# Turning queries and keys with the DMA crossbar in a fused attention and long-convolution kernel

## The chip, the core and the metric

The kernel runs on one core of a Trainium2 chip. The core has five engines with an instruction queue each: TensorE (PE in the profile; PEld is its weight load), VectorE (DVE), ScalarE (ACT), GpSimd (POOL) and SyncE (SP). Each executes its queue in order and waits on semaphores. POOL and SP also issue DMAs: POOL through a software queue, which may convert types on the way, and SP through a hardware queue. Both run on the same 16 DMA engines. The metric is device time in microseconds (us). The time before is 175.86 us, the median of three runs (175.34 to 179.3).

## What is computed

Batch 4, 8 heads, 768 positions, head size 64. The attention sees 8 global keys and a window of 96 keys back, with a bias by distance for each head. Its output, as 512 columns, passes through a gated convolution of the whole length (a Fourier transform in the reference):

```python
scores = scale * (q @ k.T) + bias          # bias = -slope[h] * distance
scores = where(keep, scores, -1e9)         # first 8 keys, or 0 <= row - col < 96
x = softmax(scores) @ v                    # (B, S, 512)
x1, x2, x3 = split(x @ w_proj)             # 512 columns each
conv = irfft(rfft(x2, axis=1) * rfft(filter_fft, axis=0))
out = ((x1 * conv * x3) @ w_out)
```

## The kernel before, in words

**Stages.** For each batch there are two parts. `attention(b)` turns queries and keys, computes scores, exponentials, masks and products with the values, normalises and turns the result into `xT`, and computes the gates (L1098) from it. `conv(b)` projects (L1159), transforms forward (L924), multiplies by the filter's spectrum, transforms back (L1181, L1184), joins with the gates and projects to the output (L1215). The work of `conv(b)` is interleaved with that of `attention(b + 1)`.

**Who sets the order.** The kernel does not leave its order to a compiler. `Plan` collects operations with their engines, estimated costs and the keys that they read and write. `lay` places them one after the other by rank, `NUDGES` shifts each operation's rank and its leaning between ACT and DVE by a stored number, and `FAVOUR` is a leaning of all. `fill` puts idle matmuls (L563, on a tile of zeros) into gaps that PE is planned to have. `program` merges the five planned lines into one program order, and `emit` writes it out. The plan knows only dependencies named by keys. When the program is written, the layer below adds the semaphore waits that it finds necessary from the memory that the instructions touch, in program order.

**Loading.** Queries, keys and values are loaded by POOL (L583), converted from 32 to 16 bits, one tile at a time: a query tile is 128 positions in `qn`, a key tile 120 positions in partitions 8 to 127 of `kn`, and a value tile likewise in `vn`. There is one `qn` and one `kn`, so the next batch's tile is loaded when the last one has been used. Of the order of a batch: query tiles 0 to 2, key tiles 0 and 1, value tiles 0 and 1; query tiles 3 and 4, key tiles 2 and 3, value tiles 2 and 3; then query tile 5, key tiles 4 to 6 and value tiles 4 to 6. Batch 0 is loaded in another way (`load_pair`) and turned by `transpose_pair`; the change does not touch its turning.

**Turning.** For batches 1 to 3, `transposes` (L931) turns a tile: four 128x128 PE transposes (L938) into one PSUM bank, then a copy by ACT or DVE (L567) into 128 columns of `QT`, or into 120 columns of the 128 that a key tile has in `KT`. The first eight columns of each of the seven key tiles hold the eight global keys. They are written by a DVE copy of their own (L949 to L951), once for each batch, which spreads the eight first keys of tile 0 over all seven tiles:

```python
g.op("V", dve(224), lambda _: self.copy(
    "V", kv[:, :, :, 0:NG], kv[:, :, 0:1, NG:2 * NG].to_broadcast([P, 4, 7, NG])),
    r=[("KT", 0)], w=["KTg"])
```

**Scores.** `scores` (L953) of a group of key tiles (0 and 1; 2 and 3; 4 to 6) for two heads reads the key tiles of its group, the query tiles they meet, and `KTg` (matmuls L975). ACT takes the exponential (L990), DVE multiplies by the mask (L997), and `values` (L1015, L1020) follows. `load_global` (L662) copies the eight global rows of the value tile for the other tiles, by SP.

**SP's queue** holds two loads of batch 0, those small value copies and the 25 output stores (L1221).

Of the kernel before, what the change touches and what calls it, by code (L numbers as in the profile page):

```python
# [17 lines left out]
NG = 8  # L18
# [46 lines left out]
class Plan:  # L65
# [90 lines left out]
    def lay(self):  # L156
# [84 lines left out]
        830, 19469, 28342, 22698, -36791, 44557, 0, 38863, 17326, 50370, 0, 17086, -14969, 46246, -10719,  # L241
        3803, 22479, 12714, -995, -27474, -4380, 3973, 17122, 3529, 7380, -663, -24781, -3497, 45666, -4551,
        -35801, 10005, 0, 12791, 0, -10379, 0, 45454, 0, -5437, 0, -14061, -19757, -14504, -37905, -18946,
        0, -32477, 0, -19819, 0, 19446, -1510, 8329, 0, 27319, 11852, 7297, -33522, -3329, -24534, -36612,
        -27852, 3113, -7029, -29691, -14381, -3884, 31147, 32034, 41013, 3882, -7384, -6372, -2549, 6629,
        68912, 8963, -61766, 5547, -44599, 12091, 18399, 14042, 6929, -4982, -7955, 13539, -24252, 20179,
        -37287, 999, -15997, -18090, 9312, 22827, 23386, 28496, -25966, 23940, -7783, 39729, 0, 1069, 0,
        12644, 0, -10150, 0, 23681, 0, -18062, 0, -19460, 0, 7837, 0, 430, 0, -3637, 0, 8913, 0, -4969, 0,
        4698, 0, 6387, -28901, -14115, 14320, -44762, 8724, -14864, 46735, -14488, 23611, -14772, -11847,
        6451, -3306, -18377, -60, 4689, 27298, 24083, -497, -18877, 16900, 19934, 37256, 19651, -14734,  # L250
        -9560, 12718, -42257, 27146, 1115, -39200, -14114, 6946, -5667, 16361, -49626, -3804, -7768, -67026,
        -18259, 60927, 21512, -46061, 5299, 29871, 21514, -44548, 5866, -12730, -23878, -15725, 33821,
        20215, -25471, 41707, 6771, 23796, 39844, 27531, -14231, -2302, -5026, 6456, 8053, 1663, -7662,
        -1658, -22536, 10581, -5577, -28542, -40863, -38468, -5794, -5468, 40622, -19008, 14370, 67736,
        -58861, 42786, 25155, -29878, -3418, 3618, 4708, -22659, -28259, -20518, 8701, 6031, -6892, -10351,
        -20996, 26804, 20150, 54288, -13311, 5794, 6136, 52867, -15428, -29665, 25192, 30956, 45334, 21269,
        43306, 2557, -24451, 6157, -1880, -4325, -2390, 7965, -31500, -28218, 18854, 4142, 15094, -27249,
        27912, 43510, -17851, -24582, -28451, 3289, -4573, 52435, 13404, 20792, -24567, 15357, -28602,
        -63577, -4124, -16002, 20822, -14047, -23587, 29959, -35143, 9243, -7310, -76644, -8134, 42347,
        15822, -12242, -3646, -30686, 275, 21750, -36005, 1469, 29713, -50088, -42560, -19350, 23864, 5050,  # L260
        -35144, 35778, -23119, -25177, 16491, -2020, 4380, -36451, -22654, -22150, -20473, 13426, -26733,
        26609, 6268, -22149, 3957, -50217, -3909, -19153, 2810, -3292, 7853, -21492, 32509, 30392, 1058,
        -3422, 15580, -35441, -9203, -35466, 64502, 42951, -19116, -24283, 2677, -62640, -12510, -59703,
        11602, 21513, 35378, 20196, 11922, -1695, 2261, 5554, -11981, 15156, 12890, -23779, -19040, -49831,
        -15466, -43761, 7442, 2473, -11475, -562, -20186, 44257, -33302, -12882, -28759, 38437, 11482, 1330,
        11240, -38355, 17055, 27903, 51476, 19276, 41100, -22953, 19243, -49765, 30962, -35331, 10963,
        42827, 51939, -23434, -11212, 50785, -4094, -27838, -30215, -24532, -12422, 67855, 13805, 3349,
        -31574, -50206, -1578, -23241, 3462, -29661, 8300, 12759, 26155, 16907, 2610, 5092, 33120, -6934,
        14181, -6832, 37905, -14123, 4017, -27020, -20812, 1598, 3482, -15360, 14795, 14629, 485, 23373,
        31416, -26303, 985, -32770, -12960, -31274, -27569, 14995, 28878, -62352, -24591, -25434, -13467,  # L270
        -1753, 33337, -31036, -11856, -18317, -11803, -33535, -27683, -51311, -11621, 1840, -23345, -13880,
        -10610, -21888, -29421, -35794, 9291, 16111, -10016, -61858, 13788, 28430, 11863, 10235, 26016,
        -11573, 27177, -20634, 32822, -31295, 24126, 16224, 34719, 32835, 36139, 40036, 830, 39163, 18794,
        23592, 7759, 51877, 15207, 11097, 5209, -31196, 47785, 18050, 12543, -18408, 3112, 9419, 28821,
        33481, 24315, -4637, -2954, 58662, 10982, 44569, -17852, -13026, 18502, 18480, 661, 39608, 43043,
        5607, -6149, 51251, -23733, 21791, 22094, 13091, 28673, -13130, 38566, 29894, 58869, 14114, 22687,
        13217, 23944, 14851, 18542, 32490, 39556, 0, 2287, 0, 19051, 0, -4358, 0, -11746, 0, 19030, -37967,
        1328, 0, -1449, 14563, -17652, -982, -19950, 0, -1349, 0, -11190, 0, 2329, 0, 1474, 0, 9498, 0,
        18549, 0, 6688, 0, 22215, 0, 20539, 0, 3845, 0, 18493, 0, -9540, 0, 5625, 0, -4323, 0, -8046, -3533,
        -19460, 16225, 5133, -15664, 1868, -10430, 13679, -822, -6032, 46722, 17, -12126, -14344, -697,  # L280
        -13742, -12505, 35119, 19976, 12563, -17553, -4315, -16313, -8060, -26919, -13513, 5645, -9234,
        -8261, 33619, 1834, -2859, -2550, 21273, 8957, -13081, -9314, 20868, 8922, -5132, 5559, 6221,
        -35799, 24500, 3519, -6685, 3949, -816, -6213, 9623, -62952, -17310, 10679, 22559, -35498, 10601,
        -12029, 6157, 5514, 7375, -48803, 10526, -28598, 4222, -27669, -30984, 26626, 10987, -54583, -53116,
        -15825, 15071, -78852, -9661, 6714, 2840, -38629, -19587, -4267, 24678, -95876, 18875, -65326,
        37035, -57223, 2718, -80355, 8544, -25562, 24290, -40863, 2118, -56826, 1618, -8022, -31710, 24818,
        3620, -25827, 27844, -44889, 2870, 4692, 1799, -40217, -9884, -31044, -26859, 10139, -30260, 15490,
        -10550, -33083, -6484, -3536, 42406, -39070, 25617, -4598, 29316, -41708, 15965, 36737, 22936,
        -38817, 8527, -48993, 22443, 17760, 28836, -35248, -5369, -32024, 12970, -29506, 46391, 21693,
        -7287, -24248, -581, -2018, 24139, -49992, 23604, -37246, -19201, -50818, 32705, -650, -7523, -9491,  # L290
        -6925, -30680, 1857, -10661, 4404, 11499, 32387, -17435, -48594, -14949, -4657, -84287, -8566,
        14498, -17867, 2527, 39846, -8706, -27278, 52664, 6571, -35366, -320, -10331, -13919, -41255,
        -14510, -27402, 30994, -7841, -31169, -15489, 10258, -20175, 13543, 2857, 2578, 131, -1314, -20053,
        -3100, 4481, -24160, -39099, 11687, -27948, -9199, -2494, 30419, -9029, -805, -6822, -33325, 13405,
        -16820, -66296, -481, -11964, 10636, -6248, -15247, -30087, 9838, -10144, -26515, -24439, -29855,
        -22320, -23621, -44190, -16823, -1332, 20402, -52166, -32146, 29136, -8657, -32420, -27767, 19595,
        4945, -41783, -6152, 22710, -839, 24762, 12982, -46639, 45086, -32249, -27885, 26993, 32349, -1139,
        -27028, 5428, -35713, -11537, -21816, 4520, 11355, -11306, -17012, 4480, -2042, -15007, 18089,
        16310, 5551, -12842, -12327, -74283, -24015, -51377, 27730, -6713, 30891, -54126, 34332, -19745,
        -18476, -68884, 4160, 17961, -25458, -47047, -23408, -74718, -25716, -25378, 10363, -21807, -25577,  # L300
        -30760, -512, -35125, -15528, 5905, 11983, -39028, 8438, -56403, -744, -68035, -9455, -28679, 15786,
        -55653, 8176, -11569, -5453, 4461, 21051, 30451, 38894, -23961, -22340, -37283, -19384, -14914, 91,
        -24447, -19426, -32077, 21216, 6861, -6808, -6892, 5217, 10775, -14628, 70698, 20491, 17063, -9496,
        43779, -27379, 19441, -35221, 40472, -6558, 6850, 27498, 19585, 24533, 14892, -3738, -53050, 27975,
        -49714, -29727, 2330, -4593, -32440, 10709, 5615, -11179, -8091, 16512, -42979, 22940, -7459,
        -19376, -58359, -5155, 3527, 14869, 75937, 14885, 50802, -44287, 9855, -3550, 31325, 23170, 11445,
# [1108 lines left out]
```

## Time and profile before

| | |
|---|---|
| median of three runs | 175.86 us (175.34 to 179.3) |
| the profiled execution | 177.28 us |
| its span in the profile | 175.5 us |
| PE busy | 166.9 us, 95% |
| DVE busy | 157.0 us, 89% |
| ACT busy | 152.6 us, 87% |
| POOL busy | 75.3 us, 43% |
| four-matmul transposes of `qn` and `kn` (L938) | 156 matmuls between 38 and 112 us |
| idle matmuls (L563) | 16, all before 12 us |
| first and last score matmuls of batch 1 | 41.7 and 60.7 us |

Times inside the profile are counted from the start of the span. The busy time of PE includes the drain of pipelined matmuls, so a PE that is shown busy may still have room. "Idle before, releaser" in a line of a group is the time that its engine stood idle before these instructions, and what ended it. DMA share above 1 means that packets of several transfers were under way on an engine at once. "To landing" is the time from the start of the instruction that issues a DMA to its completion.

### The profile page before, as it was taken

To read this page: it belongs to the slowest core of one execution; us is meant where nothing else is said; L and a number is where in the kernel's file an instruction comes from. 1 tells how busy PE (TensorE), PEld (TensorE's weight loads), DVE (VectorE), ACT (ScalarE), POOL (GpSimd) and SP (SyncE) were. 2 spreads that over 40 slices of the span, in tenths; PEclk is the share of its full clock that TensorE was granted. 3 is DMA by queue.
4 is the path that set the end of the run, shared out by engine and by line. 5 is a ranking of instruction groups with operands and counts; after the bars stand their busy time and mean duration, and the time that the engine had idled before them with its cause. 6 is when DMAs were issued, how large, how long until landed. Compare 5 with 4: busy or idle time off the path is not lost.

```text
span 175.5 us, 4566 instructions
## 1 busy us (share of the span) xinstructions
PE 166.9 (95%) x1768; PEld 104.3 (59%) x1768; DVE 157.0 (89%) x368; ACT 152.6 (87%) x304; POOL 75.3 (43%) x97
## 2 busy tenths in 40 slices
PE   7799999999899799999999999999999999999991
PEld 2357777665457567575446669754556674547540
DVE  6669778999999769999999998999899999998960
ACT  8879989999999778999997977999799897968751
POOL 7999986298997699998040300000000000000000
PEclk9999999999999999999999999999999999999998
DMA  5999999999999999999999900000710000043145
GB/s 177 148 145 134 146 200 209 166 152 138 135 166 159 132 141 142 146 144 149 66 63 344 70 4 4 0 0 0 294 70 4 0 2 4 0 159 140 60 166 197
DMA packets 79853, 20.06 MB, mean 114 GB/s; under 512 B 70528, under 2 KB 76888, under 8 KB 79832
## 3 DMA queue, kind: packets, MB, share of 16 engines
q0 software_dynamic: 75408, 12.47, 107.2%
q1 hardware_dynamic: 4424, 7.30, 11.5%
q8 instruction: 14, 0.23, 0.5%
q14 instruction: 7, 0.06, 0.1%
HBM read 25.69 MB, written 6.29 MB: 182 GB/s over the span
## 4 chain that ended last, share of the span: by engine, by line
PE 64%; DVE 14%; DMA 9%; POOL 5%; ACT 5%; issue 2%; ACTq 0%; POOLq 0%; DVEq 0%
PE bank L1098 19%; PE bank L1215 12%; DMA qn<-in_q_dram 9%; PE bank L1159 6%; PE bank L1181 4%; PE bank L1015 4%; PE bank L924 4%; PE bank L938 3%; PE bank L1020 3%; PE bank L975 3%; PE bank L1060 3%; ACT E L990 3%; POOL kn L583 2%; POOL vn L583 2%; PE bank L630 2%
## 5 line engine op out<-in xcount | busy, mean ns | idle before, releaser
L1098 PE MATMUL bank<-xT,w 128*128 128x384 f16 x256 | 45.6, 326 | 0.0
L990 ACT ACTIVATE E<-bank 128x864 f16<-128x864 f32 x48 | 41.0, 923 | 1.7 <-PE bank L975 1.3
L1098 PEld LDWEIGHTS <-w 128*128 128x128 f16 x256 | 23.9, 98 | 15.8 <-issue 0.8
L583 POOL DMA_DIRECT2D kn<-in_k_dram x24 | 21.6, 908 | 14.0 <-PE bank L938 6.6
L583 POOL DMA_DIRECT2D vn<-in_v_dram x29 | 26.2, 922 | 2.0 <-DMA w<-in_moe_w_proj_dram 1.6
L1215 PE MATMUL bank<-wo,y 128*128 128x512 f16 (+1 forms) x100 | 21.8, 371 | 0.1
L583 POOL DMA_DIRECT2D qn<-in_q_dram x21 | 18.6, 892 | 5.9 <-PE bank L755 3.2
L997 DVE TENSOR_TENSOR E<-E,mask 128x864 f16<-128x864 f16 x36 | 20.9, 597 | 0.1
L1039 DVE TENSOR_TENSOR xn<-bank,rc 128x512 f16<-128x512 f32 (+1 forms) x24 | 18.5, 775 | 0.4
L571 ACT ACTIVATE ot<-bank 128x512 f32<-128x512 f32 (+1 forms) x23 | 13.1, 606 | 5.1 <-PE bank L1215 5.0
L1108 ACT CAST g<-bank 128x384 f16<-128x384 f32 x32 | 15.7, 494 | 1.4 <-PE bank L1098 1.2
L1015 PEld LDWEIGHTS <-E 128*128 128x128 f16 x224 | 14.1, 97 | 3.6 <-DVE E L997 1.1
L571 ACT ACTIVATE ab<-bank 128x512 f16<-128x512 f32 x23 | 14.3, 633 | 2.2 <-PE bank L1159 2.0
L1215 PEld LDWEIGHTS <-y 128*128 128x128 f16 x100 | 9.5, 98 | 10.7 <-DVE y L1257 0.8
L1015 PE MATMUL bank<-vn,E 128*128 128x65 f16 x224 | 15.8, 194 | 0.0
L571 ACT ACTIVATE x<-bank 128x384 f16<-128x384 f32 x28 | 13.8, 507 | 2.3 <-PE bank L1098 1.8
L1020 PE MATMUL bank<-vn,E 128*128 128x65 f16 x192 | 15.4, 193 | 0.0
L975 PE MATMUL bank<-QT,KT 64*128 64x216 f16 (+2 forms) x224 | 15.0, 241 | 0.1
L1020 PEld LDWEIGHTS <-E 128*128 128x128 f16 x192 | 13.3, 97 | 0.4
L567 ACT CAST X<-bank 128x512 f16<-128x512 f32 x21 | 12.3, 643 | 0.0
L975 PEld LDWEIGHTS <-KT 64*128 64x128 f16 x224 | 8.3, 94 | 5.6 <-issue 3.0
L924 PE MATMUL bank<-ab,fwd 128*128 128x512 f16 x40 | 11.4, 379 | 0.0
(144 smaller groups left out, 358.2 us busy)
## 6 DMA issues: line engine op xcount, KB each, us to landing
out_dram<-ot SPq DMA_DIRECT2D x23, 256.0 KB
vn<-in_v_dram POOLq DMA_DIRECT2D x28, 120.0 KB, 6.1
kn<-in_k_dram POOLq DMA_DIRECT2D x21, 120.0 KB, 6.0
qn<-in_q_dram POOLq DMA_DIRECT2D x18, 128.0 KB, 6.7
w<-in_moe_w_proj_dram POOLq DMA_DIRECT2D x4, 256.0 KB, 7.3
g<-in_moe_filter_fft_dram POOLq DMA_DIRECT2D x1, 768.0 KB, 12.5
qn<-in_q_dram POOLq DMA_DIRECT2D x3, 192.0 KB, 5.0
kn<-in_k_dram POOLq DMA_DIRECT2D x3, 192.0 KB, 5.1
```

What stands on the lines that cost most here:

```text
L571: self.nc.scalar.mul(out, in_, c)
L583: return self.g.op(eng, 0.57 + 0.00035 * nbytes[0] if eng == "G" else 0.5, lambda _: e.dma_start(dst, src), w=w, r=r, nbytes=nbytes, name= ...
L924: self.nc.tensor.matmul(b.f32(), self.fwd[:, f], src(i, t), start=(n == 0), stop=(n == len(terms) - 1))
L975: nc.tensor.matmul(bs[hh].f32()[:, off:off + w], self.KT[hs, hp, P * m:P * m + P], self.QT[hs, hp, KL * m:KL * m + w], start=(off == 0 and ...
L990: g.op("A", act(864), lambda _: nc.scalar.activation(eo, bs[0].two()[:, :, 0:432].rearrange("p h (m w) -> p h m w", m=2), Act.Exp, scale=s ...
L997: g.op("V", dve(864, 2), lambda _: nc.vector.tensor_mul(eo, eo, mk), r=[("E", hp, gi), ("mask", hp)], w=[("E", hp, gi)], name="masked")
L1015: nc.tensor.matmul(o[:, n, hh], ef[:, at:at + P], vt[:, t, 2 * hp + hh, :], start=first, stop=(t == 0), skip_group_check=True)
L1020: nc.tensor.matmul(o[:, n, hh], ef[:, at:at + P], vt[:, t - 1, 2 * hp + hh, :], start=False, stop=True, skip_group_check=True)
L1039: nc.vector.tensor_mul(to, o[:, :, :, 0:D], rc.to_broadcast([P, 2, 2 * nt, D]))
L1098: nc.tensor.matmul(bk.f32()[:, 0:h], self.w[:, c, o + P * j:o + P * j + P], self.xT[:, c, h * s:h * s + h], start=(c == 0), stop=(c == 3))
L1108: g.op("A", act(h), lambda _: nc.scalar.copy(x3, pts[1].f32()[:, 0:h]), use=[pts[1]], w=[ko], name="x3")
L1215: nc.tensor.matmul(bk.f32()[:, 0:n], y[:, c, P * t:P * t + P], self.wo[:, c, cs], start=(c == 0), stop=(c == 3))
```

## The change

The turning of 31 of the 39 tiles of batches 1 to 3 moves from PE to a DMA. A new set `CROSS` names them: all query and key tiles of batches 2 and 3, and key tiles 2 to 6 of batch 1. For these, SP issues one `dma_start_transpose` each, which reads the tile in `qn` or `kn` (128 partitions, 512 columns) and writes 128 columns of `QT` or `KT` in four blocks. The PSUM bank, the four matmuls and the copy of the tile fall away.

Since a crossbar DMA writes all 128 columns of a key tile, the eight global ones too, batches 2 and 3 get their global keys beforehand: `load_global` now also copies the eight rows of key tile 0 in `kn` to the other tiles, and the DVE copy of `KTg` is left out for these two batches. In batch 1, key tiles 0 and 1 are still turned by PE and the DVE copy of `KTg` stays.

The planner's numbers change beside it: a new table `NUDGES`, `FAVOUR` from 0.1 to 0.0, the lead that `fill` allows for in the first gap from 2.2 to 2.0 us (so that there are 24 idle matmuls and not 16), and the planned size of a packet in batch 0's loads. The new order also hands some copies from one of ACT and DVE to the other.

```diff
-    FAVOUR = 0.1
+    FAVOUR = 0.0
...
-                gap = o.start - at - 2.2 * (at < BEGIN + 1.0)
+                gap = o.start - at - 2.0 * (at < BEGIN + 1.0)
...
+    CROSS = frozenset((b, w, t) for b in (1, 2, 3) for w in "qk" for t in range(7)
+                      if b > 1 or w == "k" and t > 1)
...
-            0, hs].rearrange("h (p r) d -> p h (r d)", r=6), [(what + "n", "pair", hp)], (256, 1536), what)
+            0, hs].rearrange("h (p r) d -> p h (r d)", r=6), [(what + "n", "pair", hp)], (256, 1990), what)
...
-                self.load_global(vt, s)
-
-    def load_global(self, vt, s):
+                self.load_global(vt, ("vng", s), ("vn", s, 0), ("vn1", s))
+
+    def load_global(self, tile, key, *r):
         for c, (t, n) in enumerate(((0, 2), (2, 5))):
-            self.load("S", vt[0:NG, t:t + n], vt[NG:2 * NG, 0:1].to_broadcast(
-                [NG, n, self.H, self.D + 1]), [("vng", s, c)], (8 * n, 1040), "vglobal",
-                r=[("vn", s, 0), ("vn1", s)])
+            self.load("S", tile[0:NG, t:t + n], tile[NG:2 * NG, 0:1].to_broadcast(
+                [NG, n, self.H, tile.shape[-1]]), [key + (c,)], (8 * n, 1040), "global", r=r)
...
+    def turned(self, b, what, t, src, cols):
+        if (b, what, t) not in self.CROSS:
+            self.transposes(what, t, src, cols)
+            return
+        dst = (self.QT if what == "q" else self.KT)[:, :, cols:cols + P]
+        keys = [("kng", min(t // 2, 1))] if what == "k" else []
+        self.g.op("S", 1.3, lambda _: self.nc.sync.dma_start_transpose(
+            out=dst, in_=src.rearrange("p h d -> p (h d)")), r=[(what + "n", t)] + keys,
+            w=[(what.upper() + "T", t)], nbytes=(512, 650), name=what + "T")
+        if what == "k" and t == 0:
+            self.g.writer["KTg"] = self.g.writer[("KT", 0)]
...
-                    self.transposes("q", t, self.qn[:, t], P * t)
+                    self.turned(b, "q", t, self.qn[:, t], P * t)
...
-                    self.transposes("k", t, self.kn[:, t], P * t)
+                    self.turned(b, "k", t, self.kn[:, t], P * t)
...
+                if t == 0 and (b, "k", 0) in self.CROSS:
+                    self.load_global(self.kn, ("kng",), ("kn", 0))
```

## The prediction

> **What bounds the kernel now.** I read the 40 slices first (no long hole: PE, DVE and ACT all near full from 10 us on), then busy time by stage, then the order in time around 41 us. Stages: us, then busy us of PE, weight load, DVE, ACT and POOL, granted clock, DMA share, GB/s.
>
> ```profile
> 40.00:60.00 20.00, 18.18 (x210) 10.87 (x208) 18.52 (x45) 18.77 (x32) 16.70 (x19) 1.00 2.54 149
> 60.00:167.00 107.00, 106.68 (x1044) 66.62 (x1042) 102.81 (x217) 95.25 (x183) 26.43 (x30) 1.00 0.75 84
> ```
>
> From 60 to 167 us PE (106.7 of 107) and DVE (102.8) are both full, so an engine held up before 60 us has no slack later. The DMA engines are crowded until about 98 us (share 2.54) and idle soon after.
>
> Three engines' lines in order of time, at the first scores of batch 1 (start, length, engine, line):
>
> ```profile
> 40.84 0.21 DVE L567 COPY KT<-KT 128x224 f16<-128x224 f16 x1
> ```
> ```profile
> 41.70 0.55 PE L975 MATMUL bank<-QT,KT 64*128 64x216 f16 x8
> ```
> ```profile
> 41.01 2.71 POOL L583 DMA_DIRECT2D kn<-in_k_dram  x3
> ```
>
> The DVE copy spreads the eight global keys over all seven key tiles of KT; every score matmul of the batch reads it, and 0.86 us after its start the scores begin. But POOL issues the loads of key tiles 4, 5 and 6 only now. Their time to landing, from the issues in a narrow window at 42.7 us (the other tile is the one before):
>
> ```profile
> kn<-in_k_dram POOLq DMA_DIRECT2D x2, 120.0 KB, 6.5
> ```
>
> So tile 6, issued third at 41.01 + 2 x 0.90 = 42.8 us, lands at 49.3 us. Before, that hurts nobody: only the third group of scores needs tiles 4 to 6.
>
> **The change, part by part.**
>
> *The turns taken off PE.* 31 of 39 groups of four L938 transposes go. Merged, four take 0.22 us (20 took 1.12 us in the chain): 31 x 0.22 = 6.8 us of PE, 1.1 of it between 40 and 60 us, 5.7 after.
>
> *Copies from PSUM.* Their durations:
>
> ```profile
> L567 ACT COPY KT<-bank 128x480 f16<-128x480 f16 x15 | 8.8, 604 | 0.6 <-PE bank L938 0.6
> L567 ACT COPY QT<-bank 128x512 f16<-128x512 f16 x13 | 8.0, 626 | 0.5 <-PE bank L938 0.5
> L567 DVE COPY KT<-bank 128x480 f16<-128x480 f16 x6 | 2.3, 396 | 0.0
> L567 DVE COPY QT<-bank 128x512 f16<-128x512 f16 x5 | 2.1, 418 | 0.9 <-PE bank L938 0.9
> ```
>
> The new nudges reassign other copies too, so I counted each form in both built programs and multiplied by these rows. ACT loses 15 KT copies and 9 QT copies (14.7 us) and, with what it takes over and gives away, falls by 11.4 us (its eight new 128x64 products have no row; I took the 64x64 row's 0.245 us; 0 or twice that is 2 us either way on the engine with most room). DVE loses four KT, three QT and two global copies (3.3 us), hands four eo, two X and several batch-0 copies to ACT and takes five ab copies of 0.68 us: net 6.0 us less. But 3.1 of these lie in batch 0's part, before 20 us; 2.9 us fall after 41 us. A tuned order thus gains at most about 3 us where DVE limits and 6.8 where PE does.
>
> *The wait that comes.* The crossbar writes whole 128-column tiles of KT, the eight global columns included. For batches 2 and 3 the global keys are copied into kn beforehand by small DMAs, and the DVE copy is gone. For batch 1 tiles 0 and 1 still go through PE, and the DVE copy stays. It writes columns that five crossbar transposes (key tiles 2 to 6) write as well. The plan has no edge between the two, but in the built program the transposes stand ahead of the copy and the copy waits for five hardware-DMA semaphores, exactly those transposes' counts, tile 6's among them. So it cannot start before tile 6 has landed (49.3 us) **and** been turned. DVE executes in order: behind it stand three gate products, the second key copy, the filter's folds (L861 to L873) and all masks; PE's first score matmul waits for the copy and the rest of PE's order stands behind that, ACT's exponentials behind PE. All three stop.
>
> How long? Let x be issue to landing of the crossbar DMA; no row shows one. Rows to bound it: 3.6 us (120 KB load issued at 96 us, quiet DMA) and 8.8 us (the same issued at 50 to 52 us, crowded). SP's own queue has one usable row: ot is loaded with an issue at 0.74 us and its cast starts at 5.23, at most 4.5 us for 384 KB. I take 4.5: same queue, more bytes, but fewer rivals. Nothing excludes less than 3.6; zero would still leave 49.3 us. SP's hold per issue is 0.45 us for a load; tiles 4 to 6 land 0.95 us apart, so a hold up to 0.95 adds nothing and twice that adds 2 us, inside x's upper end. The copy then starts at 49.3 + 4.5 = 53.8 us instead of 40.84, and the scores at 53.8 + 0.86 = 54.7 instead of 41.70: **13.0 us late**.
>
> *What is made up.* Work left from there, if an engine never waited again. PE: 16.5 us (18.18 less the 1.7 before 41.7) - 1.1, then 106.7 - 5.7, then the last 8.5 us as they are: 124.9; from 54.7, an end at 179.6. DVE: 17.7 (18.52 less 0.84) + 102.8 - 2.9 + 8.5 = 126.1; from 53.8, 179.9. So the floor is 179.9, 4.4 above 175.5. The waits would have to vanish for that: DVE idled 1.5 us in the first stage and 4.2 in the second. Loads run on during the stop, so waits like PE's 1.0 us for qn go; waits of DVE and PE for each other need not. I count 2.3 of the 5.7.
>
> *Clock.* PE stands still for some 12 us. At the start, eleven 128x512 idle matmuls took 4.88 us, about 430 ns apart, against about 220 in later groups (24 of L1215 in 5.35). I count 1 us; 0 if ACT's exponentials (0.83 us per pair of heads) hide it, 2 at most. The Trainium skill's "TensorE: Matmul & The Clock Gate", Part 1: The HAM clock gate, says that an idle window of about 3.4 us halves PE's clock and as long a busy one restores it. The granted clock of this profile reads 1.00 even in those first slices, so only the spacing of the matmuls agrees. By that rule the loss would be an estimated 1.7 us, and the sum 0.7 higher.
>
> *Edits with small answers.* Sixteen idle matmuls become 24: the one added in the first group ends before qn lands at 7.09 us (first PE gap 1.02 us); the two in the second stand on the chain (0.97 us for two), 0.9 us; the rest lie in planned gaps. With FAVOUR and the 2.6 us of copies moved to ACT in batch 0, the front may be 0 to 2.5 us later, but the stop's end is set by the loads, so it disappears there; without the stop it would count. The 1990 and 650 are planner's costs and move only the order. The four kn copies (SP's vn ones hold it 0.70 us) and the 26 transposes of batches 2 and 3 run in SP's order before and between the six first outputs; PE reaches those scores 10 us later than now, their loads do not, so the extra transfers hide. If that cover went, PE would wait at the first scores of batch 2 or 3: 0 to 5 us (one crowded landing less the quiet one). I take 0.
>
> The Trainium skill's "VectorE: DVE Perf Modes", The three transpose paths, speaks against the change by itself: 390 ns for a 128x128 turn on TensorE, 1309 ns through the DMA crossbar. The row on this trace is 55 ns per turn in a pipelined group plus a 0.4 to 0.6 us copy per four. If the four blocks of one DMA ran singly at the page's figure, an estimated 5.2 us would stand for x and the sum would be 0.7 higher.
>
> **Sum.** 175.5 + 4.4 + 2.3 + 1 = 183.2, say +7.5 us. The profiled execution took 177.28 (1.8 around its span), which gives 184.8; it lay 1.4 above the median of the runs, so against 175.86 I predict **183.4 us**.
>
> **Rivals.**
> 1. *The stop is short and the relief whole*: x = 3.6, no waits beyond the floor, no clock loss: 179.9 - 0.9 = 179.0, +3.5, or 179.4: the border. With PE's and DVE's old idle going too it is 177 to 179, no change. For it: DMA has 12 us to run ahead. Against: DVE's waits are spread over the whole second stage. 0.12.
> 2. *The crossbar is slow in the crowd*: x = 8.8, all 5.7 us of waits stay, clock 2: 183.2 + 4.3 + 3.4 + 1 = 192. For: loads issued just then take 8.8 us. Against: its own queue. 0.14.
> 3. *Faster*: the wait costs nothing and the relief alone counts: 175.9 less 3 to 6.8, about 171. It needs tile 6 turned by 41 to 43 us, when DVE reaches the copy; from 45 us on the relief is eaten up. Against: the load itself lands at 49.3, and its place in POOL's order is unchanged. 0.04.
> 4. My forecast, 180 to 187: 0.70.
>
> Runs differ by about 2% (175.34 to 179.3), so within 2% is 172.3 to 179.4. Slower: 0.70 + 0.14 and a little of the first rival, 0.86; same 0.10; faster 0.04. The range leaves out most of the second rival's end and the third: 178.5 to 190.
>
> **What would show it.** In the changed profile: the DVE copy KT<-KT (128x224, now once) idle before it by about 12 us with a DMA as releaser, starting near 54; a hole in PE, DVE and ACT from 42 to 54 us; the L938 transposes (L935 in the changed file) x32 in place of x156; PE full after 56. The forecast is wrong if that copy starts before 46 us, if the crossbar DMAs slow the loads of batch 3 until PE waits for KT or QT after 100 us, or if the engines after the stop run no denser than now.

## The result

The changed kernel takes **192.54 us** (median of four runs, 191.35 to 193.91); beside it the kernel before took 176.16 us (175.34 to 179.3). The ratio is 1.095, with a 95% interval of 1.085 to 1.105: slower by 16.7 us. (Here and below a ratio and its interval leave out runs more than 1.5% above the fastest of the same kernel; medians in us are of all runs.) I had predicted 183.4 us, at most 190. The direction and the wait that I named are there; its length is not.

The profiled execution of the changed kernel took 193.91 us, its span is 192.1 us. First the slices of the page (PE and its granted clock), and two stages with the columns of the prediction's first fence.

```profile
PE   7995988996000899999998999998999999999992
PEclk9999699999855589999999999999999999999998
```
```profile
40.00:60.00 20.00, 6.56 (x54) 4.08 (x52) 5.06 (x12) 7.11 (x14) 13.63 (x16) 0.78 2.11 131
60.00:167.00 107.00, 101.73 (x1005) 60.07 (x1006) 99.77 (x210) 87.62 (x165) 29.92 (x33) 0.96 1.38 111
```

Between 40 and 60 us PE is busy for 6.6 us where it was busy for 18.2; DVE and ACT stop with it. The hole is deeper and longer than the 42 to 54 us that I expected, and the granted clock falls to 0.5 in it.

The first scores of batch 1, in DVE's and in PE's order of time (the bracket is the idle time before and what ended it), and the waits of both:

```profile
44.42 0.67 DVE L856 TENSOR_TENSOR g<-pp 128x1024 f16<-128x1024 f16 x1
61.89 0.22 DVE L565 COPY KT<-KT 128x224 f16<-128x224 f16 x1 [16.79 <-DMA KT<-kn]
```
```profile
46.17 0.39 PE L935 MATMUL bank<-ident,qn 128*128 128x128 f16 x4
62.16 0.36 PE L984 MATMUL bank<-QT,KT 64*128 64x216 f16 x2 [15.61 <-DVE KT L565]
```
```profile
PEld L984 <- DVE KT L565: 16.8, 2, 15.8
DVE KT L565 <- DMA KT<-kn: 16.8, 1, 16.8
```

This is the copy of the global keys (L567 before, L565 now). It waits 16.8 us for a crossbar transfer, PE waits for it, and the scores start at 62.2 us in place of 41.7, 20.5 us late. From there to the end it is 129.9 us; before it was 133.8. So 3.9 us were made up, and the span is 16.6 us longer.

What set the time of the copy is in the chain that ended last (start, length, what):

```profile
41.62 1.80 POOL kn L581 x2
43.42 7.45 DMA kn<-in_k_dram
50.92 10.69 DMA KT<-kn
61.89 0.22 DVE KT L565
```

Key tile 6 is issued at 43.42, lands at 50.9 and is then under way in the crossbar transfer for **10.7 us**. I had put 49.3 and 4.5.

### The profile page after: what moved, and what is told of

Same layout as the page of the kernel before. It is cut to its first block, busy times and chain, and to the rows that moved or that the text cites. A ratio compares the mean times of both kernels' runs of the same rounds, so it can differ in the third digit from the quotient of the medians.

```text
span 192.1 us, 4396 instructions
## 1 busy us (share of the span) xinstructions
PE 164.8 (86%) x1652; PEld 98.8 (51%) x1652; DVE 150.0 (78%) x354; ACT 145.8 (76%) x292; POOL 74.8 (39%) x97
## 3 DMA queue, kind: packets, MB, share of 16 engines
q1 hardware_dynamic: 21432, 11.49, 31.7%
## 4 chain that ended last, share of the span: by engine, by line
PE 50%; DMA 29%; POOL 8%; ACT 4%; issue 3%; DVE 3%; SPq 1%; ACTq 0%; POOLq 0%; DVEq 0%
DMA KT<-kn 14%; PE bank L1107 12%; PE bank L1224 10%; DMA vn<-in_v_dram 8%; PE bank L1168 6%; PE bank L921 5%; DMA kn<-in_k_dram 4%; POOL kn L581 4%; PE bank L984 3%; DMA vn<-vn 3%; PE bank L1190 3%; ACT E L999 2%; PE bank L1069 2%; PE bank L1024 2%; PE bank L975 2%
## 5 line engine op out<-in xcount | busy, mean ns | idle before, releaser
L999 ACT ACTIVATE E<-bank 128x864 f16<-128x864 f32 x48 | 41.5, 906 | 23.0 <-PE bank L984 23.0
L1107 PE MATMUL bank<-xT,w 128*128 128x384 f16 x256 | 44.9, 326 | 0.0
L984 PE MATMUL bank<-QT,KT 64*128 64x216 f16 (+2 forms) x224 | 17.0, 256 | 18.0 <-DVE KT L565 16.4
L581 POOL DMA_DIRECT2D qn<-in_q_dram x21 | 18.7, 895 | 21.0 <-PE bank L1069 8.7
L984 PEld LDWEIGHTS <-KT 64*128 64x128 f16 x224 | 8.8, 98 | 26.4 <-DVE KT L565 16.8
L1048 DVE TENSOR_TENSOR xn<-bank,rc 128x512 f16<-128x512 f32 (+1 forms) x23 | 17.8, 773 | 0.3
L1024 PE MATMUL bank<-vn,E 128*128 128x65 f16 x224 | 15.5, 193 | 2.2 <-DMA vn<-vn 2.0
L1029 PE MATMUL bank<-vn,E 128*128 128x65 f16 x192 | 15.0, 193 | 0.0
L565 DVE COPY KT<-KT 128x56 f16<-128x56 f16 (+1 forms) x5 | 1.5, 323 | 17.2 <-DMA KT<-kn 16.8
L565 ACT CAST X<-bank 128x512 f16<-128x512 f32 x23 | 13.6, 626 | 0.6 <-PE bank L921 0.6
L565 ACT CAST eo<-bank 128x384 f16<-128x384 f32 x29 | 12.2, 495 | 0.8 <-PE bank L1193 0.7
```

The lines of the kernel that those rows point to most:

```text
L565: {"A": nc.scalar.copy, "V": nc.vector.tensor_copy, "G": nc.gpsimd.tensor_copy}[e](out, in_)
L581: return self.g.op(eng, 0.57 + 0.00035 * nbytes[0] if eng == "G" else 0.5, lambda _: e.dma_start(dst, src), w=w, r=r, nbytes=nbytes, name= ...
L984: nc.tensor.matmul(bs[hh].f32()[:, off:off + w], self.KT[hs, hp, P * m:P * m + P], self.QT[hs, hp, KL * m:KL * m + w], start=(off == 0 and ...
L999: g.op("A", act(864), lambda _: nc.scalar.activation(eo, bs[0].two()[:, :, 0:432].rearrange("p h (m w) -> p h m w", m=2), Act.Exp, scale=s ...
L1024: nc.tensor.matmul(o[:, n, hh], ef[:, at:at + P], vt[:, t, 2 * hp + hh, :], start=first, stop=(t == 0), skip_group_check=True)
L1029: nc.tensor.matmul(o[:, n, hh], ef[:, at:at + P], vt[:, t - 1, 2 * hp + hh, :], start=False, stop=True, skip_group_check=True)
```

## The experiments

### Parts of the change, in an order that the planner made anew

Four kernels changed only `CROSS`, or the copy, left the planner to lay out the order, and kept each stored nudge with the operation that it was made for. The first three have the old numbers of the kernel before (`NUDGES`, `FAVOUR`, lead, packet size):

```diff
 # b1_only
+    CROSS = frozenset((1, "k", t) for t in range(2, 7))
 # b23_only
+    CROSS = frozenset((b, w, t) for b in (2, 3) for w in "qk" for t in range(7))
 # b3_only
+    CROSS = frozenset((3, w, t) for w in "qk" for t in range(7))
```

> The kernel before, with its own planner's numbers and its own idle matmuls; only key tiles 2 to 6 of batch 1 go through the crossbar (5 of the 31 transfers), and the DVE copy that spreads the global keys waits for all five. Theory A (the whole loss is this one wait): the copy starts at 60 to 62 us as in the changed kernel, the first scores of batch 1 at 61 to 63 instead of 41.70, and since only 5 x 0.22 = 1.1 us of turns leave PE, no more than 5 us of the 20 are made up: 189 to 194 us. Theory B (the 26 transfers of batches 2 and 3, or the new planner's numbers, hold a good part of the loss): the copy starts at 54 or before, the total is below 186.

> The kernel before, with its own planner's numbers and its own idle matmuls; only batches 2 and 3 go through the crossbar (26 of the 31 transfers), so batch 1 has no crossbar transfer and the DVE copy of its global keys waits for nothing new. Theory A (the loss is batch 1's wait): no stop between 42 and 54 us, 5.7 us of turns leave PE, and the total is 171 to 177 us, not slower than before. Theory B (the crossbar transfers crowd the DMA engines, so that batch 2's or 3's keys and queries come late): holes in PE after 60 us with a DMA as releaser, and 181 us or more.

> The kernel before, with its own planner's numbers and its own idle matmuls; only batch 3 goes through the crossbar (14 transfers, whose input is loaded when the DMA engines are nearly idle). Theory A: 14 groups of turns less on PE (3.1 us), nothing late: 172 to 176 us. Theory B (crossbar transfers are late even with quiet DMA engines): PE waits for KT or QT at batch 3's first scores, 177 to 182 us. The time from issue to landing of these transfers is the quiet bound for x: A under 5 us, B 7 or more.

The fourth takes the wait out of the changed kernel. Its copy no longer touches what the crossbar writes:

```diff
 # mended
-                "V", kv[:, :, :, 0:NG], kv[:, :, 0:1, NG:2 * NG].to_broadcast([P, 4, 7, NG])),
+                "V", kv[:, :, 0:2, 0:NG], kv[:, :, 0:1, NG:2 * NG].to_broadcast([P, 4, 2, NG])),
...
+                if t == 0 and b == 1:      # one DMA: rows of key tile 0 to tiles 2 to 6 of kn
+                    self.load_global(self.kn, ("kng",), ("kn", 0), cs=(1,))
```

> The changed kernel with all 31 crossbar transfers, except that the DVE copy of batch 1's global keys now writes tiles 0 and 1 alone and tiles 2 to 6 get the global keys through kn by one small DMA, as batches 2 and 3 do; the copy no longer waits for the crossbar. Theory A (the loss is that wait): the first scores of batch 1 start near 46 us (the front is 4.2 us later than before, which then counts), later ones wait tile by tile, and the total is 178 to 185 us. Theory B (the transfers' traffic and the late tiles themselves cost as much as the wait): PE stops at the first scores that read tiles 2 to 6 and the total stays at 188 or more.

Measured: b1_only 218.31 us, b23_only 204.07, b3_only 189.40, mended 200.43. b1_only and b3_only lie beyond both theories, b23_only and mended under theory B's "or more"; and taking the wait out made the changed kernel slower, not faster. (Batch 3 has 13 such tiles, not the 14 of its expectation.) The stop itself was there as expected in b1_only (the copy at 62.51 us, after 20.9 us idle), but the rest of these times cannot be read. The stored nudges belong to one list of operations; with another list they still gave an order, but an untuned one: by the traces, hundreds of PE's some 1700 matmuls stand elsewhere in its order in each. These runs tell of the edit and of a new order at once. So I wrote out the order of each engine and the PSUM banks of both kernels as a list, and made the edits in that. The lists hold the order: in the trace of warm_stop, a run further down that adds 66 idle matmuls, all but one of PE's other 1652 stand in the order that they have in the changed kernel's trace.

### The same parts in a fixed order

fixed_b1, fixed_b23 and fixed_b3 are the kernel before; the named turns and copies are struck from the list, and the transfer stands in SP's queue at the place of the copy. fixed_mended is the changed kernel with the edit of mended.

> The kernel before with every engine's instructions and PSUM banks held in its own order (a written list instead of the planner); the only edit: the turns of batch 1's key tiles 2 to 6 leave PE, their copies leave DVE and ACT, and five crossbar transfers stand in SP's queue in their place. Theory A (the wait of the DVE copy is the whole loss): the copy starts at 60 to 62 us, PE's first scores of batch 1 at 61 to 63 instead of 41.70, 20 us late, of which the 5.7 us of PE's and DVE's later waits, less the slow clock after the stop, are made up: 189 to 196 us. Theory B (part of the changed kernel's loss is the crossbar traffic of batches 2 and 3): the same stop, but 182 to 188. Theory C (the 218 us measured with the planner's own order for this edit was the edit and not the order): 210 or more.

Measured: 195.56 us, ratio 1.106 (1.098 to 1.115). Theory A: in the profiled execution (209.27 us) the copy started at 60.6 us and the first scores at 60.9, and five transfers, added to the kernel before, cost 18.7 us, about as much as the whole change. That the wait of the copy is all of it does not follow, since the five tiles are late here as well. The 23 us from here to b1_only are the order.

> The changed kernel in its own fixed order, with the one edit that takes the wait away: the DVE copy of batch 1's global keys writes tiles 0 and 1 alone, and one small DMA ahead of the crossbar transfers brings the global keys of tiles 2 to 6 into kn. Theory A (the loss is this wait): PE's first scores of batch 1 start near 46 us, those that read tiles 2 to 6 wait until these land (53 to 61 us, as in the changed kernel), so a part of the stop stays: 181 to 187 us. Theory B (the late tiles alone hold the order up as long as the wait does): 190 to 195. Theory C (nothing but the copy ever waited): 176 to 180.

Measured: 183.08 us, ratio 1.039 (1.032 to 1.046); theory A. Of the 16.7 us the wait of the copy is 9.8, as the difference of the two kernels, and 6.9 stay. PE's scores begin at 42.73 and run until they need tiles that are still being turned:

```profile
42.73 0.54 PE L813 MATMUL bank<-QT,KT 64*128 64x216 f16 x8
53.69 0.27 PE L813 MATMUL bank<-QT,KT 64*128 64x216 f16 x2 [2.57 <-DMA KT<-kn]
55.91 0.36 PE L813 MATMUL bank<-QT,KT 64*128 64x216 f16 x2 [1.96 <-DMA KT<-kn]
```

> As the kernel before in its own fixed order, with batch 3's 13 turns alone replaced by crossbar transfers (its loads come when the DMA engines have become quiet). Theory A: 2.9 us of turns less on PE, no wait: 172.5 to 176 us. Theory B: x is 6.5 us even with quiet DMA engines, and PE waits for batch 3's keys: 177 to 183.

> The kernel before in its own fixed order, with the turns of batches 2 and 3 (26) replaced by crossbar transfers at the copies' places in the order, and the global keys brought into kn by four small DMAs. No wait is added in batch 1. Theory A (the transfers hide, 0 to 1 us of waits, and 5.7 us of turns leave PE): 170 to 176 us. Theory B (a transfer takes 6.5 us or more where turn and copy took about 1.5, and the order asks for the tiles 1 to 2 us after the copy's place): PE waits for KT or QT in batches 2 and 3, several us each: 180 to 192.

Measured: fixed_b3 188.96 us, ratio 1.073 (1.063 to 1.083); fixed_b23 205.67 us, ratio 1.162 (1.151 to 1.173). Both lose far more than theory B allowed, and for another reason than its 6.5 us in the quiet. SP's queue of fixed_b3 (start, length, instruction), and what PE did then:

```profile
115.08 1.21 SPq L784 DMA_TRANSPOSE QT<-qn  x1
116.39 1.22 SPq L784 DMA_TRANSPOSE KT<-kn  x1
117.66 1.26 SPq L784 DMA_TRANSPOSE QT<-qn  x1
118.96 3.88 SPq L784 DMA_TRANSPOSE KT<-kn  x3
122.88 1.27 SPq L784 DMA_TRANSPOSE QT<-qn  x1
```
```profile
115.14 0.81 PE L936 MATMUL bank<-xT,w 128*128 128x384 f16 x4
125.50 1.26 PE L813 MATMUL bank<-QT,KT 64*128 64x216 f16 x12 [9.54 <-DMA QT<-qn]
```

Each transfer here holds SP for 1.2 to 1.3 us, the next one starts only then, and PE, whose order has nothing else to run at this place, waits 9.5 us for the last. PE's own turn of a tile costs 0.22 us and a copy beside it. At the old copies' places the transfers stand in one row with nothing for PE beside them. In the changed kernel's order they cost far less (fixed_no_b1, below), so these two runs tell what the new order is for, not what batches 2 and 3 cost in it.

They also hold the number that I had lacked. The issues of fixed_b23 (last figure: median us from issue to landing), first from 62 to 75 us, then from 125 to 140:

```profile
KT<-kn SPq DMA_TRANSPOSE x2, 8.1
```
```profile
KT<-kn SPq DMA_TRANSPOSE x7, 2.4
```

POOL's loads run in the first stretch (DMA share 2.56) and none in the second (0.37): 8.1 against 2.4 us.

### Is it the crowd? Holding POOL's loads back

In held_loads POOL copies a piece of the turned tile 6 before it issues the next load:

```diff
+            self.g.op("G", 0.1, lambda _: self.nc.gpsimd.tensor_copy(
+                self.hold, self.KT[:, 0, 896 - 64:896 - 56]), r=[("KT", 6)], name="hold")
```

> The changed kernel in its own fixed order with one instruction more: behind the load of batch 1's key tile 6, POOL copies 8 columns of the turned tile 6, so its next loads (values of batch 1, the output weights, batch 2) are held until the five crossbar transfers have landed, and the transfers have the DMA engines to themselves. Theory A (x is long because other loads crowd the DMA engines; quiet transfers took 2.4 us in fixed_b23): tile 6, issued near 51 us, lands 2.4 to 3.5 us later, the DVE copy starts at 53.5 to 55, the total falls to 184 to 188 us. Theory B (x is long because five transfers stand behind each other, or by itself): the copy still starts at 59 us or later, 191 or more. Theory C: x falls as in A, but the loads that were held are then late and take the gain back: copy near 54, total 189 or more.

The chain and DVE's order of held_loads:

```profile
43.62 6.63 DMA kn<-in_k_dram
50.30 2.45 DMA KT<-kn
```
```profile
53.04 0.22 DVE L396 COPY KT<-KT 128x224 f16<-128x224 f16 x1 [10.81 <-DMA KT<-kn]
```

And a stretch of time while tile 6 was under way, first of held_loads, then of the changed kernel (columns as in the stages above; the last two are the DMA share and GB/s):

```profile
50.00:52.00 2.00, 0.00 (x0) 0.00 (x0) 0.00 (x0) 0.00 (x0) 0.00 (x0) 0.50 0.63 126
```
```profile
50.00:54.00 4.00, 0.00 (x0) 0.00 (x0) 0.00 (x0) 0.00 (x0) 2.49 (x3) 0.65 3.16 108
```

The same transfer, fifth of the same five, takes 2.45 us at a DMA share of 0.63 and 10.69 at 3.16. Theory B, a slow or queued crossbar, has fallen. More bytes did not move in the crowd (108 GB/s against 126); whether the loads slow the transfer by their many small packets or in another way was not tested. The total was 188.07 us, ratio 1.058 (1.045 to 1.070): by the two ratios 6.6 us less than the changed kernel, of the 8.9 by which the copy starts earlier. A part of theory C is in it too: from the first scores (53.31) to the end it is 133.1 us here, 129.9 in the changed kernel. PE waits 3.0 us for a key tile at 97.8 us, where after the stop of the changed kernel no such wait is longer than 0.9; this fits the loads that were held and came later, and how much of the 3.2 us they make was not measured.

> Both mendings in the changed kernel's fixed order: the DVE copy writes tiles 0 and 1 alone and waits for no crossbar transfer, and POOL's loads behind batch 1's last key tile are held until tile 6 is turned. Theory A (the two costs add: the wait and the crowd): PE's waits for batch 1's key tiles fall from 8 us to 2 or 3, 177 to 181 us. Theory B (holding the loads makes batch 1's values or batch 2 late): 183 or more, no better than the one mending alone.

Measured: 191.16 us, ratio 1.081 (1.072 to 1.089): theory B, and worse than either mending alone. Batch 1 runs without a stop (PE is busy for 17.5 of 18 us from 42 to 60), but POOL stood for 12.2 us, and so batch 2's keys are late:

```profile
56.59 0.39 POOL L796 COPY hold<-KT 128x8 f16<-128x8 f16 x1 [12.20 <-DMA KT<-kn]
```
```profile
75.76 1.46 PE L945 MATMUL bank<-xT,w 128*128 128x384 f16 x8
88.29 0.36 PE L822 MATMUL bank<-QT,KT 64*128 64x216 f16 x2 [11.06 <-DMA KT<-kn]
```

Held in this way, the loads are out of the transfers' way in batch 1 and late in batch 2.

### Batches 2 and 3 alone, in the changed kernel's order

fixed_no_b1 gives batch 1's five tiles back to PE (copies: three ACT, two DVE), at places in the changed kernel's list where a PSUM bank is free.

> The changed kernel in its own fixed order, but batch 1's key tiles 2 to 6 are turned on PE and copied by ACT (3) and DVE (2) as before; batches 2 and 3 go through the crossbar. Theory A (all of the loss is batch 1's part: the wait of the copy, 9.4 us by fixed_mended, and the late tiles themselves): no stop between 46 and 63 us, 173 to 178 us. Theory B (batches 2 and 3 cost by their own late tiles, as they did in the order of the kernel before): PE waits for KT and QT after 100 us, and the total is 180 or more.

Measured: 179.51 us, ratio 1.017 (1.011 to 1.023), between the two theories. The copy starts at 42.19 and the first scores at 43.70, 2.0 us later than before; from there to the end it is 133.7 us, before 133.8. So on balance the 26 turns that PE no longer does brought nothing, and a late tile of batch 2 is in the chain, with a wait of PE behind it:

```profile
43.70 0.55 PE L815 MATMUL bank<-QT,KT 64*128 64x216 f16 x8
```
```profile
78.15 10.21 DMA KT<-kn
```
```profile
88.41 0.64 PE L815 MATMUL bank<-QT,KT 64*128 64x216 f16 x10 [2.17 <-DMA KT<-kn]
```

With this the 16.7 us divide: 9.8 for the copy's wait (the whole less fixed_mended's 6.9), 3.9 for batch 1's late tiles themselves (6.9 less 3.0), 3.0 for the rest, of which the later front is 2.0. Each of the three is a difference of ratios and uncertain by 1 to 2 us.

### The clock after the stop

warm_stop puts 66 idle matmuls ahead of batch 1's first scores in PE's order.

```diff
-390P7 276G 366P45
+390P7 276G ~66:4 366P45
```

This is the written list: number of the operation, engine, PSUM banks. 366 is the first group of scores of batch 1, `~66:4` the idle matmuls, in bank 4.

> The changed kernel in its own fixed order with 66 idle matmuls (128x512, some 14.5 us) in PE's order ahead of batch 1's first scores, so that PE keeps running while it waits; they end before the DVE copy does. Theory A (the halved clock after the stop, 0.50 from 51.5 to 68.9 us, costs 2.5 us or more): 188 to 190.5 us, granted clock 1.00 throughout. Theory B (the slow matmuls after the stop lie beside ACT's exponentials and DVE, as my prediction's lower bound had it): 191.5 to 193.5, the same as the changed kernel.

Measured: 191.14 us, between the two theories. By the ratio, 1.076 (1.067 to 1.084) against 1.095 (1.085 to 1.105), it is some 3.4 us less than the changed kernel, the intervals just apart; by the medians of all runs it is 1.4 us. The two runs with a mean granted clock of 0.99 took 189.38 and 190.12 us, the three with 0.979 to 0.982 took 191.14 to 193.68. This leans to theory A and does not show it, for the cover was not whole: in the profiled execution (192.47 us) the copy waited 19.2 us, the idle matmuls ended before it, and the granted clock was 0.70 from 62 to 70 us, where it was 0.61 in the changed kernel. How much a clock of 1.00 throughout would bring stays open.

## Why the prediction was wrong

*What limits.* Right. With PE and DVE full from 60 us on, an early stop was not absorbed: 16.6 of 20.5 us reached the end.

*The wait.* Right in place and kind: one DVE copy, held by the hardware DMA of key tiles 2 to 6, with PE's scores and ACT's exponentials behind it. fixed_mended shows that it was the largest part.

*Tile 6 lands at 49.3.* It landed at 50.9, 1.6 us later: 7.45 us after its issue, which itself came 0.6 us later.

*x = 4.5: this step failed.* It measured 10.7, above my upper bound of 8.8 as well. I had taken a load at the very start of the kernel as the nearest row because it goes through SP's queue, and written "fewer rivals". The queue is SP's own, the DMA engines are not. held_loads gives 2.45 us without rivals, so x lay below my lower row (3.6) or above my upper one, by what POOL was loading. I had the two rows for that, a load in the quiet at 3.6 and one in the crowd at 8.8, and chose between them by the queue and not by the DMA share from 40 to 60 us, which was 2.54. With x = 10.7 and the landing at 50.9 in place of 49.3 my own sum would have given 183.2 + 1.6 + 6.2 = 191.0 for the span, against 192.1.

*What is made up, and the clock.* From the first scores to the end I had 128.5 us and it was 129.9. The relief is there: DVE is busy 7.0 us less in all (predicted 6.0), ACT 6.8 less (predicted 11.4; ACT was not what limited). Why ACT's relief is the smaller stays open. The price of the clock lies between nothing and some 3 us, and my 1 is neither confirmed nor refuted: after the first scores at 62.16 the granted clock stayed at 0.50 for 6.1 us, in which at most half the time was lost, and warm_stop does not show how much of it ACT's exponentials hide. The Trainium skill's "TensorE: Matmul & The Clock Gate", Part 1, with its idle window of about 3.4 us, agrees roughly with what the granted clock shows here. It fell 4.6 us after PE's last matmul in the changed kernel and 3.2 in held_loads, and rose 6.1 and 3.9 us after PE had begun again; the stretches at 0.50 lasted 17.07 and 10.24 us, and 6.83 in warm_stop, which is five, three and two times 3.41.

*Batches 2 and 3 hide: 0.* Right with the stop, in whose 20 us the loads run ahead: PE's waits for crossbar tiles after it sum to 1.5 us. Without the stop it fails: in fixed_no_b1 they eat up the relief of 26 turns (5.7 us of PE). I had named this price, 0 to 5, and the front's 0 to 2.5, which measured 2.0.

*SP's hold.* I had 0.45 us of a load, took a hold up to 0.95 as free and twice that as 2 us. It is 1.2 to 1.3 us for 24 of the 31 transfers of the changed kernel, as the 1.3 in the planner's cost of a transfer (`self.g.op("S", 1.3`) could have told me, and 1.6 to 3.2 for the others, 2.30 for tile 6. It delayed nothing there: the transfer ahead of tile 6's, issued at 49.23, held SP until 50.48, and tile 6 landed at 50.9. In fixed_b3 the hold set the end.

*The rule on transposes.* From the figure of the Trainium skill's "VectorE: DVE Perf Modes", The three transpose paths, I had estimated 5.2 us for x. Neither state measured that: 2.45 in the quiet, 10.7 in the crowd. The measurement decides, and no single figure stands for x.

*The rivals.* The total is that of the second, 192. Its mechanism, the crowd, was the right one; of its terms x was still too small by 1.9, tile 6 landed 1.6 later than it had it, and the waits that it kept were partly made up. These errors cancel, so that the total fits as well as it does is in part luck.

## What to carry to other kernels

Price a transfer by what else the DMA engines move at that moment, not by the queue that issues it: the same 128 x 512 turn took 2.45 us alone and 10.7 us among loads. A helper that writes whole tiles also writes the columns that another engine fills; look for the wait that this adds, and for who stands behind it. To test one part of a kernel whose order is tuned, hold the order fixed: the same edit measured 200 us in an order made anew and 183 in the changed kernel's own.

## What the runs showed of the hardware

- A crossbar transfer from SBUF to SBUF of 128 x 512 two-byte elements holds SP for 1.2 to 1.3 us in most cases (the changed kernel's medians: 1.27 us for KT, 1.21 for QT), up to 3.24 us among loads, and puts some 550 packets into the DMA engines: the hardware queue has 21432 packets where it had 4424, for 31 transfers and four small copies.
- From its issue to its landing it took 2.45 us at a DMA share of 0.63 and 10.69 at 3.16.
- Loads beside it were slow too: in the changed kernel two loads of key tiles, issued at 51.2 and 53.0 us, had a median of 12.4 us to landing, where two issued between 50 and 52 us took 8.8 before. That the transfers did this was not tested.
- In the profiles of the changed kernel, held_loads and warm_stop the granted clock was 1.00 or 0.50, and around the stop it was 0.50 for 17.07, 10.24 and 6.83 us: whole multiples of 3.41 us.
